# An attention block in which the score matmuls take all 128 rows of the array

## The chip, the cores and the metric

The kernel runs on one core of one Trainium2 chip. The metric is the device time of an execution in microseconds (us). Several executions are timed, and the median counts; one execution more is recorded by the hardware profiler, and its trace is what the profile and its views are read from.

Engines are named as in the profile: PE is TensorE (PEld are its weight loads), DVE is VectorE, ACT is ScalarE, POOL is GpSimd, SP is SyncE, which here only issues transfers. L188 is line 188 of the kernel.

## The reference, cut to what matters

The output mixes an attention block and a gated feed-forward block by a gate per token. There are 2048 tokens of width 448, and 16 heads of width 28.

```python
def _A_ref(x, wqkv, wo):                      # S = 2048, D = 448, H = 16, Dh = 28
    q, k, v = qkv[0], qkv[1], qkv[2]          # of x @ wqkv, by head
    scores = einsum("bhqd,bhkd->bhqk", q, k) * (Dh ** -0.5)
    p = softmax(scores)
    return einsum("bhqk,bhkd->bhqd", p, v) ... @ wo

def _B_ref(x, W_gate, W_up, W_down):          # F = 1792
    gate, up = x @ W_gate, x @ W_up
    return (gate * (gate > 0) * up) @ W_down

g = sigmoid((x * gate_w).sum(-1, keepdims=True))
return g * a + (1 - g) * b                    # a, b: the two blocks
```

## The kernel before

**Exactness by parts.** Most products are made in a faster 32-bit form of matmul with each operand split into a high part and a remainder. A projection is a chain of 11 matmuls (`TERMS`), issued at L341 for q and k and at L359 for v. The gate and up products of the feed-forward block are chains of the same kind at L510, the down product is at L770, the output projection at L725.

**Heads.** A head has only 28 rows, so four products of parts lie one below the other: `K[h % 3]` holds in rows 0 to 111 the parts high, low, high, low of k, and `Q[h]` the parts high, high, low, low of q. `GD` is 4 x 28 = 112. One matmul over 112 rows thus gives the sum of the four products. K has three buffers, Q three (tag "Q"). The rows 96 to 127 of each K buffer are filled with -1 at the start; the loads of a head overwrite rows up to 111, so rows 112 to 127 stay -1.

**Row maxima and scores.** For each head there are two passes over the 2048 x 2048 scores.

- `smax` (L188, L189): queries as weights, keys as moving data, 112 rows, into a bank of PSUM; VectorE reduces each 128 x 512 piece to maxima. There are 64 pieces a head. When a head is done, the maxima are transposed and split into two parts, which two small transfers on POOL's queue (L204) put into rows 112 and 113 of `Q[h]`.
- `scores` (L214, L216): keys as weights, queries as moving data, 114 rows. The two rows of maxima times the -1 in K subtract the maximum inside the product. ScalarE takes the exponential out of PSUM. There are 64 pieces a head, too.

The product with v follows per round (`pv`, L544) in column tiles of 32.

**Order.** The order of work on TensorE is written out by hand in strings of letters (`ROUNDS`): s is a matmul of scores, m one of row maxima, x one of gate or up. In most rounds they alternate. The row maxima run ahead of the scores by 24 tiles of keys and more. Weights for x come through `fetch_f` (SP's queue, L230) and are split by ScalarE and POOL.

**Loads of a head.** `load_k` (L174) and `load_q` (L179) issue four transfers each on SP's queue, 28 rows of 8 KB each. Heads 0, 1 and 2 are loaded during the projections and the first round; head h + 2 is loaded when the scores of head h begin, once the buffers of head h - 1 are free. SP issues its transfers in order.

**Start.** VectorE fills a small piece of V with zeros (L383); 11 matmuls on it keep TensorE going until data has come (L386). POOL then makes the identity, fills K with -1 (L393) and two columns of V per group (L395, L396), and is next used when the first q and k parts go out to DRAM (L348).

Of the kernel before, what the change touches and what calls it, by code (L numbers as in the profile page):

```python
# [8 lines left out]
F32 = mybir.dt.float32  # L9
# [9 lines left out]
P = 128  # L19
S = 2048  # L20
# [4 lines left out]
GD = G * DH  # L25
# [3 lines left out]
TB = 512  # L29
# [49 lines left out]
def gated_mix_kernel(ctx, tc, x, wq, wo, wgu, wd, out):  # L79
    nc = tc.nc  # L80
# [4 lines left out]
    dram = ctx.enter_context(tc.tile_pool(name="dram", bufs=1, space=DRAM))  # L85
# [4 lines left out]
    def f32(ap):  # L90
        return ap.bitcast(F32)
# [8 lines left out]
    def turn(kind, among):  # L100
        count[kind] = count.get(kind, -1) + 1
        return among[count[kind] % len(among)]
# [4 lines left out]
    def ps_x():  # L107
        return banks[turn("x", (4, 5))]
# [35 lines left out]
    x_d = {(tb, r): dram.tile([P, 4, TB], F32, name=f"x_d_{tb}_{r}") for tb in range(1, NB) for r in range(2)}  # L144

    v_d = {g: dram.tile([P, NK, 4, 32], F32, name=f"v_d_{g}") for g in (2, 3)}

    l_d = [dram.tile([NB, TB], F32, name=f"l_d_{h}") for h in range(H)]
    o_d = dram.tile([D, S], F32, name="o_d")
# [9 lines left out]
    V = vp.tile([P, 4, NK, 4, 32], F32, name="V")  # L159
    K = [vp.tile([P, S], F32R, name=f"K{r}") for r in range(3)]  # L160

    def p_slot(k, name, dt=F32):
        if k in (5, 6):
            return V[:, k - 3].rearrange("p k h d -> p (k h d)").rearrange("p (j t) -> p j t", t=TB)
        return (vp if k < 5 else att).tile([P, 4, TB], dt, name=name, tag=f"P{k}", bufs=1)
# [4 lines left out]
    Q = {}  # L170
# [5 lines left out]
    def load_q(h):  # L176
        Q[h] = q_slot(f"Q_{h}").rearrange("p j t -> p (j t)")
        for r in range(4):
            nc.sync.dma_start(f32(Q[h])[DH * r:DH * (r + 1)], qk_d[r // 2, 2 * DH * h + DH:2 * DH * (h + 1), :])  # L179

    MX, M = {}, {}

    def smax(k, ps):

        h, u, c = k // (4 * NK), k // 4 % NK, k % 4
        if u == 0 and c == 0:
            MX[h] = keep.tile([P, 64], F32, name=f"mx_{h}", tag="mx", bufs=2)
        nc.tensor.matmul(ps, Q[h][:GD, u * P:(u + 1) * P], K[h % 3][:GD, c * TB:(c + 1) * TB], start=True, stop=True)  # L188
        nc.vector.tensor_reduce(MX[h][:, 4 * u + c:4 * u + c + 1], ps, axis=AX.X, op=OP.max)  # L189
        if u == NK - 1 and c == 3:  # L190
            M[h] = keep.tile([P, 16], F32, name=f"m_{h}", tag="m", bufs=2)
            nc.vector.tensor_reduce(M[h], MX.pop(h).rearrange("p (a b) -> p a b", b=4), axis=AX.X, op=OP.max)
# [17 lines left out]
    def scores(i, j, ps):  # L210
        h, kt = divmod(i, NK)
        if j == 0:
            PT[i] = p_slot(i % NP, f"P_{i}")
        nc.tensor.matmul(ps, K[h % 3][:GD + 2, kt * P:(kt + 1) * P], Q[h][:GD + 2, j * TB:(j + 1) * TB],  # L214
                         start=True, stop=True)
        nc.scalar.activation(PT[i][:, j], ps, AF.Exp, scale=SCALE)  # L216

# [15 lines left out]
    with tc.tile_pool(name="qkv", bufs=1) as pa:  # L233
# [147 lines left out]

        warm = V[:, 3, 0:2].rearrange("p k h d -> p (k h d)").bitcast(BF16)
        nc.vector.memset(warm, 0.0)  # L383
        ps = ps_x()
        for n in range(WARM):
            nc.tensor.matmul(ps, warm[:, :P], warm, start=True, stop=True)  # L386
# [48 lines left out]
        for n, (f, *a) in enumerate(mixed):  # L435
            if n == 0:
                split_w(*w5)
            if n == 6:
                load_k(1)
                load_q(1)  # L440
            if n == 8:
                split_w(*w3)
            if n == 13:

                nc.gpsimd.memset(f32(K[2])[96:128], -1.0)
            if n == len(mixed) - 6:
                fetch_f(0)
            if n in spills:
                spill_x(*spills[n])

            among, ends = [], m
            while n >= first and m < (n + 1 - first) * ahead / (len(mixed) - first):
                among.append((smax, m, ps_w()))
                m += 1
            news = [(scores, *divmod(k, NB), ps_s()) for k, back in enumerate(EARLY) if back == len(mixed) - n]
            for k, c in enumerate(news):
                among.insert(2 * k + 1, c)
            f(*a, among=among)

            if 0 in M and ends >= 4 * NK:  # L460
                for part in smax_end(0, ps_x()):
                    part()
# [139 lines left out]
    for r, (order, nu) in enumerate(ROUNDS):  # L602
# [13 lines left out]
        for o in order:  # L616
            if o in "sS":
                i, j = i0 + ns // NB, ns % NB
                if j == 0 and i % 4 == 0:
                    small_things(i // 4)  # L620
                if len(EARLY) <= i * NB + j:
                    scores(i, j, ps_late(o) if o == "S" else ps_p() if late else ps_s())
                ns += 1
                if rest and ns > 2:
                    rest.pop(0)()
            elif o in "mM":
                smax(m, ps_late(o) if o == "M" else ps_w() if r == 0 and nm < 4 else ps_m())
                m += 1
                nm += 1
# [3 lines left out]
            elif o == "x":  # L633
                i, half, k = passes.pop(0)
# [3 lines left out]
                if k == NT - 1:  # L638
                    i, half, ps = units.pop()
# [231 lines left out]
```

## Time and profile before

| | us |
|---|---|
| median of 3 runs | 1284.22 |
| lowest and highest run | 1283.09, 1286.48 |
| the profiled execution | 1283.81 |
| its span in the profile | 1282.0 |

| engine | busy us | instructions |
|---|---|---|
| PE | 1275.8 | 6687 |
| PEld | 922.6 | 6687 |
| DVE | 895.3 | 1364 |
| ACT | 778.2 | 1424 |
| POOL | 371.2 | 563 |

Busy time is the time in which at least one instruction of the engine was under way. Matmuls overlap, one starting before the last has ended, so a busy TensorE does not tell the pace; for that the distance between starts is read. In a row of the groups, "112*128 112x512" stands for 112 rows and 128 columns of the array and 512 columns of moving data, then follow the count, the busy time of the group and the mean duration of one.

### The profile page before, as it was taken

The page shows a single profiled execution, that of the slowest core. Times are in us where ns is not written, and L with a number is a line of the kernel's source. Part 1 is how long each engine was busy: PE and PEld are TensorE (multiplying, and loading weights), DVE is VectorE, ACT ScalarE, POOL GpSimd, SP SyncE. Part 2 cuts the span into 40 slices and gives each one's busy share as a digit, 9 for nine tenths or more (in the row PEclk, how much of TensorE's full clock was granted, in tenths as well). Part 3 has the DMA queues.
Part 4 walks back from the last instruction along what each step waited for, and adds up shares of the span by engine and source line. Part 5 has one row for each costly group of instructions (what it writes and reads, how often), then busy time and mean ns, then how long its engine had stood idle before and what let it go on. Part 6 is the DMA issues. An engine that isn't in the chain of part 4 may idle for free.

```text
span 1282.0 us, 18203 instructions
## 1 busy us (share of the span) xinstructions
PE 1275.8 (100%) x6687; PEld 922.6 (72%) x6687; DVE 895.3 (70%) x1364; ACT 778.2 (61%) x1424; POOL 371.2 (29%) x563
## 2 busy tenths in 40 slices
PE   9999999999999999999999999999999999999998
PEld 6888866677666676666766667766677666899997
DVE  6598768798777897777977779877788314753342
ACT  5212767686766786677867668766787774322121
POOL 3222222412333122423133331324222443641020
PEclk9999999999999999999999999999999999999999
DMA  9936443133144314141444323142331225644432
GB/s 314 297 148 243 138 128 94 63 83 102 59 120 159 75 43 115 66 107 43 123 109 131 97 60 90 52 115 66 91 107 47 86 84 176 203 129 158 133 114 79
DMA packets 53569, 148.89 MB, mean 116 GB/s; under 512 B 10024, under 2 KB 17128, under 8 KB 48872
## 3 DMA queue, kind: packets, MB, share of 16 engines
q1 hardware_dynamic: 36120, 98.34, 26.9%
q0 software_dynamic: 16928, 48.93, 10.6%
q8 instruction: 52, 0.85, 0.3%
q10 hardware_dynamic: 432, 0.46, 0.1%
q14 instruction: 37, 0.30, 0.1%
HBM read 102.06 MB, written 46.02 MB: 116 GB/s over the span
## 4 chain that ended last, share of the span: by engine, by line
PE 99%; DMA 0%; ACT 0%; DVE 0%; SPq 0%; issue 0%; ACTq 0%
PE b L510 22%; PE b L214 19%; PE b L188 19%; PE b L544 17%; PE b L770 10%; PE b L341 6%; PE b L359 3%; PE b L725 3%; DMA wr<-wq 0%; PE b L196 0%; DVE wg L136 0%; ACT wg L130 0%; SPq L293 0%; DVE y L776 0%; ACT W L130 0%
## 5 line engine op out<-in xcount | busy, mean ns | idle before, releaser
L189 DVE TENSOR_REDUCE mx<-b 128x1 f32<-128x512 f32 x1024 | 685.7, 688 | 28.7 <-PE b L188 20.4
L216 ACT ACTIVATE P<-b 128x512 f32<-128x512 f32 x840 | 493.9, 599 | 153.8 <-PE b L214 84.6
L510 PE MATMUL b<-X,wg 128*128 128x512 f32 (+1 forms) x1232 | 438.1, 400 | 0.3 <-DVE wg L136 0.3
L214 PE MATMUL b<-Q,K 114*128 114x512 f32 x1024 | 406.9, 397 | 0.0
L188 PE MATMUL b<-K,Q 112*128 112x512 f32 x1024 | 403.7, 397 | 0.0
L510 PEld LDWEIGHTS b<-X,wg 128*128 128x128 f32 (+1 forms) x1232 | 222.5, 189 | 58.7 <-issue 9.5
L214 PEld LDWEIGHTS b<-Q,K 114*128 114x128 f32 x1024 | 194.4, 190 | 55.0 <-issue 12.6
L188 PEld LDWEIGHTS b<-K,Q 112*128 112x128 f32 x1024 | 193.1, 189 | 48.6 <-DVE mx L189 2.7
L544 PE MATMUL b<-P,V 128*32 128x512 f32 x1680 | 188.2, 593 | 0.0
L139 POOL TENSOR_TENSOR wg<-wgr,wg 128x384 fp32r<-128x384 f32 x200 | 143.4, 732 | 9.8 <-issue 1.6
L544 PEld LDWEIGHTS b<-P,V 128*32 128x32 f32 x1680 | 52.6, 110 | 121.2 <-issue 118.7
L770 PE MATMUL b<-WD,hh 128*128 128x448 f32 x672 | 138.5, 365 | 0.0
L532 POOL DMA_DIRECT2D h_d<-h x56 | 31.4, 562 | 363.0 <-DVE h L526 312.0
L770 PEld LDWEIGHTS b<-WD,hh 128*128 128x128 f32 x672 | 126.2, 188 | 10.3
L216 ACT ACTIVATE V<-b 128x512 f32<-128x512 f32 x184 | 107.9, 600 | 41.5 <-PE b L214 26.8
L130 ACT ACTIVATE hh<-hr 128x512 fp32r<-128x512 f32 x56 | 35.4, 631 | 124.4 <-PE b L770 120.2
L136 DVE TENSOR_TENSOR hh<-hr,hh 128x512 fp32r<-128x512 f32 x56 | 50.1, 894 | 66.1 <-ACT hh L130 66.1
L341 PE MATMUL b<-X,W 128*128 128x512 f32 x308 | 84.3, 398 | 0.6 <-ACT X L130 0.6
L550 DVE TENSOR_TENSOR os<-b,os 128x512 f32<-128x512 f32 x16 | 11.1, 692 | 86.1 <-PE b L544 86.1
L341 PEld LDWEIGHTS b<-X,W 128*128 128x128 f32 x308 | 57.9, 189 | 15.4 <-DVE X L136 1.7
L559 POOL DMA_DIRECT2D l_d<-rs x16 | 9.0, 561 | 203.5 <-DVE rs L558 203.5
L548 DVE COPY os<-b 128x512 f32<-128x512 f32 x16 | 11.1, 691 | 78.5 <-PE b L544 78.5
(70 smaller groups left out, 710.9 us busy)
## 6 DMA issues: line engine op xcount, KB each, us to landing
wgr<-wgu SPq DMA_DIRECT2D x55, 512.0 KB
K<-qk_d SPq DMA_DIRECT2D x64, 224.0 KB
Q<-qk_d SPq DMA_DIRECT2D x64, 224.0 KB
h_d<-h POOLq DMA_DIRECT2D x56, 256.0 KB, 2.6
hr<-h_d SPq DMA_DIRECT2D x56, 256.0 KB
qk_d<-st POOLq DMA_DIRECT2D x21, 512.0 KB, 3.6
x_d<-X POOLq DMA_DIRECT2D x6, 1024.0 KB, 5.1
X<-x_d SPq DMA_DIRECT2D x24, 256.0 KB
```

The costliest lines, as they stand in the source:

```text
L136: nc.vector.tensor_tensor(dst, src, f32(high), op=OP.subtract)
L139: nc.gpsimd.tensor_tensor(dst, src, f32(high), op=OP.subtract)
L188: nc.tensor.matmul(ps, Q[h][:GD, u * P:(u + 1) * P], K[h % 3][:GD, c * TB:(c + 1) * TB], start=True, stop=True)
L189: nc.vector.tensor_reduce(MX[h][:, 4 * u + c:4 * u + c + 1], ps, axis=AX.X, op=OP.max)
L214: nc.tensor.matmul(ps, K[h % 3][:GD + 2, kt * P:(kt + 1) * P], Q[h][:GD + 2, j * TB:(j + 1) * TB], start=True, stop=True)
L216: nc.scalar.activation(PT[i][:, j], ps, AF.Exp, scale=SCALE)
L341: nc.tensor.matmul(ps, W[:, a, c * P:(c + 1) * P], xf(tb, b), start=(n == 0), stop=(n == NT - 1))
L359: nc.tensor.matmul(ps[:, :VC], xf(tb, b)[:, t * P:(t + 1) * P], W[:, a, 2 * D:2 * D + VC], start=(n == 0), stop=(n == NT - 1))
L510: nc.tensor.matmul(ps, WS[i][rows, s, a], xf(i // NF, b)[rows], start=(n == 0), stop=(n == NT - 1))
L544: nc.tensor.matmul(po[32 * j:32 * j + 32], V[:, h // 4 % 2, i % NK, h % 4], p[:, j], start=(i == i0), stop=(i == i0 + ni - 1))
L725: nc.tensor.matmul(ps[:, :D], ON[tb][b // 4][:, b % 4, t * P:(t + 1) * P], WO[:, a], start=(n == 0), stop=(n == NT - 1))
L770: nc.tensor.matmul(ACC[i // NF][t][:, :D], HH[i][:, a, t * P:(t + 1) * P], WD[:, f, b], start=(f == 0 and n == 0), stop=(f == NF - 1 and n ...
```

## The change

The matmuls of `smax` and of `scores` read all 128 rows of K and Q in place of the first 112 and 114. Rows 112 to 127 of K hold -1 as before. Rows 112 to 127 of Q, which held no defined values but the maxima, are filled with zeros with each load of a head, by a fifth transfer on SP's queue, which reads a row of zeros in DRAM (`z_d`) 16 times. That row is written once at the start by a transfer on POOL's queue, from the zeros that VectorE has put into V for the first matmuls. The maxima are later written over rows 112 and 113 as before.

```diff
+    z_d = dram.tile([1, S], F32, name="z_d")
...
         for r in range(4):
             nc.sync.dma_start(f32(Q[h])[DH * r:DH * (r + 1)], qk_d[r // 2, 2 * DH * h + DH:2 * DH * (h + 1), :])
+        nc.sync.dma_start(f32(Q[h])[GD:], z_d[0:1].to_broadcast([P - GD, S]))
...
-        nc.tensor.matmul(ps, Q[h][:GD, u * P:(u + 1) * P], K[h % 3][:GD, c * TB:(c + 1) * TB], start=True, stop=True)
+        nc.tensor.matmul(ps, Q[h][:, u * P:(u + 1) * P], K[h % 3][:, c * TB:(c + 1) * TB], start=True, stop=True)
...
-        nc.tensor.matmul(ps, K[h % 3][:GD + 2, kt * P:(kt + 1) * P], Q[h][:GD + 2, j * TB:(j + 1) * TB],
+        nc.tensor.matmul(ps, K[h % 3][:, kt * P:(kt + 1) * P], Q[h][:, j * TB:(j + 1) * TB],
                          start=True, stop=True)
...
         nc.vector.memset(warm, 0.0)
+        nc.gpsimd.dma_start(z_d.rearrange("a (p c) -> (a p) c", p=8), V[:8, 3, 0:2].rearrange("p k h d -> p (k h d)"))
```

The order of the instructions on TensorE, VectorE and ScalarE is the same before and after. SP has 16 transfers more, POOL one.

## The prediction

> **What bounds the kernel now.** I read the page first: the busy shares, the granted clock, the chain that ended last. Then I read the groups by line with shapes kept apart, and last the timeline, since a change in the shape of a matmul is paid for in the distance from one start to the next.
>
> ```profile
> span 1282.0 us, 18203 instructions
> ...
> PE 1275.8 (100%) x6687; PEld 922.6 (72%) x6687; DVE 895.3 (70%) x1364; ACT 778.2 (61%) x1424; POOL 371.2 (29%) x563
> ...
> PEclk9999999999999999999999999999999999999999
> ...
> PE 99%; DMA 0%; ACT 0%; DVE 0%; SPq 0%; issue 0%; ACTq 0%
> PE b L510 22%; PE b L214 19%; PE b L188 19%; PE b L544 17%; PE b L770 10%; PE b L341 6%; PE b L359 3%; PE b L725 3%; DMA wr<-wq 0%; PE b L196 0%; DVE wg L136 0%; ACT wg L130 0%; SPq L293 0%; DVE y L776 0%; ACT W L130 0%
> ```
>
> TensorE is busy for all but 6.2 us of the span, at the full granted clock, and the chain that sets the end runs through it for 99%. The two lines that the change rewrites, L188 and L214, hold 38% of that chain. So two things can move the time: a different pace of these matmuls, or a new wait in front of TensorE. Work on other engines and queues costs nothing as long as TensorE never waits for it.
>
> **Term 1: the matmuls get 128 rows.** The change replaces 1024 matmuls of 112 rows and 1024 of 114 rows by as many of 128 rows. Columns stay at 512, weight columns at 128, and the order of instructions on TensorE is the same, so no instruction is added there.
>
> ```profile
> L510 PE MATMUL b<-X,wg 128*128 128x512 f32 x1136 | 421.7, 396 | 0.3 <-DVE wg L136 0.3
> L214 PE MATMUL b<-Q,K 114*128 114x512 f32 x1024 | 406.9, 397 | 0.0
> L188 PE MATMUL b<-K,Q 112*128 112x512 f32 x1024 | 403.7, 397 | 0.0
> L510 PEld LDWEIGHTS b<-X,wg 128*128 128x128 f32 x1136 | 215.3, 190 | 50.0 <-DVE mx L189 1.5 <-DVE wg L136 0.9 <-issue 0.8
> L188 PEld LDWEIGHTS b<-K,Q 112*128 112x128 f32 x1024 | 193.1, 189 | 48.6 <-DVE mx L189 2.7
> ```
>
> A matmul of 128 rows lasts 396 ns, one of 114 or 112 rows 397; the weight loads last 190 and 189. By duration the row count is free. But matmuls overlap, so duration is not pace. For pace I take two stretches of 20 us with no column-tiled work in them: at 18 us every matmul has 128 rows, at 300 us the three shapes alternate. The first two rows are stretches (length, busy time and instructions by engine, granted clock, DMA share, GB/s), the others are the TensorE groups inside them.
>
> ```profile
> 18.00:38.00 20.00, 20.00 (x88) 16.20 (x87) 13.20 (x20) 10.96 (x20) 6.44 (x9) 1.00 1.00 362
> 300.00:320.00 20.00, 20.00 (x87) 16.18 (x86) 19.67 (x30) 17.06 (x29) 0.00 (x0) 1.00 0.40 93
> ...
> L341 PE MATMUL b<-X,W 128*128 128x512 f32 x88 | 20.6, 395 | 0.0
> ...
> L510 PE MATMUL b<-X,wg 128*128 128x512 f32 x29 | 11.5, 397 | 0.0
> L214 PE MATMUL b<-Q,K 114*128 114x512 f32 x29 | 11.5, 396 | 0.0
> L188 PE MATMUL b<-K,Q 112*128 112x512 f32 x29 | 11.5, 396 | 0.0
> ```
>
> 88 against 87: with the 0.40 us that the last one hangs over, 20.4/88 = 232 ns against 20.4/87 = 234.5 ns, and one matmul more or less at an edge is 2.7 ns. So the paces agree as closely as this can say. Longer runs of starts are sharper (rows of the timeline, and two of the chain, "8.07" and "1075.10"):
>
> ```profile
> 10.80 27.47 PE L341 MATMUL b<-X,W 128*128 128x512 f32 x117
> ...
> 300.17 0.40 PE L510 MATMUL b<-X,wg 128*128 128x512 f32 x1
> 300.40 0.39 PE L188 MATMUL b<-K,Q 112*128 112x512 f32 x1
> 300.63 0.40 PE L214 MATMUL b<-Q,K 114*128 114x512 f32 x1
> ...
> 302.97 0.40 PE L510 MATMUL b<-X,wg 128*128 128x512 f32 x1
> ...
> 1087.58 5.20 PE L510 MATMUL b<-X,wg 128*128 128x512 f32 x22
> ...
> 8.07 30.20 PE b L341 x126
> ...
> 1075.10 10.21 PE b L510 x44
> ```
>
> The mix: twelve starts from 300.17 to 302.97, 233.3 ns each; a step out of 128 rows, one out of 112 and one out of 114 all take 0.23 to 0.24. Full rows alone: (27.47 - 0.40)/116 = 233.4 ns early in the kernel, 10.21/44 = 232.0 and (5.20 - 0.40)/21 = 228.6 near the end. The early stretch, nearest in kind since the other engines and the DMAs are at work around it, gives the pace of the mix to 0.1 ns. I take 0 for this term. Its bounds: a gain if the mix went at the fastest full-row pace, 234.5 - 228.6 = 5.9 ns; a loss if the new matmuls went at the slowest full-row stretch shown, 30.20/126 = 239.7 ns (which holds start-up waits), so 5.2 ns.
>
> **Term 2: sixteen zero loads on SP's queue.** Each head's load of Q gets a fifth transfer, 16 rows of 8 KB, 128 KB, behind its four of 224 KB. The maxima of a head now need it too. Head 0 has the least room:
>
> ```profile
> Q<-qk_d SPq DMA_DIRECT2D x64, 224.0 KB
> ...
> 42.87 4.41 SPq L174 DMA_DIRECT2D K<-qk_d  x4
> 48.66 3.52 SPq L179 DMA_DIRECT2D Q<-qk_d  x4
> ...
> SPq L179 <- DMA Q<-qk_d: 3.6, 4, 1.4
> ...
> 52.88 0.19 PEld L188 LDWEIGHTS b<-K,Q 112*128 112x128 f32 x1
> ```
>
> The four Q loads of head 1 (48.66) were each held until a Q load of head 0 had landed (the waits row). Their issues end at 48.66 + 3.52 = 52.18; with 0.44 us for one issue (1.76/4 in a row further down) the last left at 51.74, so head 0's Q was in by then, and one follows another at (3.52 - 0.44)/3 = 1.03 us. The zeros come next in the queue, where K of head 1 was (42.87). At 128/224 of 1.03 us they land 0.59 us later, at 52.33; the first weights of L188 are read at 52.88. They fit by 0.55 us: cost 0. If they took as long as a whole load they would land at 52.77 and still fit; two loads long would cost 0.9 us.
>
> The Trainium skill, "SBUF — State Buffer", section on the DMA port swizzle, says that bandwidth follows the number of ports that the partitions reach, and that 16 partitions reach four, with 104 GB/s measured. By that the transfer would take 1.26 us, an estimate from that page, the zeros would land at 53.00, and the sum would be 0.1 us more. No row of this trace has a 16-partition load of this size.
>
> Later heads have room:
>
> ```profile
> 284.31 0.22 DVE L192 TENSOR_REDUCE m<-mx 128x16 f32<-128x64 f32 x1
> ...
> 255.69 1.76 SPq L179 DMA_DIRECT2D Q<-qk_d  x4
> 290.33 0.36 SPq L230 DMA_DIRECT2D wgr<-wgu  x1
> ```
>
> Head 4's Q is issued at 255.69 to 257.45. Its first maximum comes after head 3's maxima are closed at 284.31. In SP's queue nothing goes out after that load until 290.33. A transfer of 0.44 us issue and 0.6 us data disappears in 27 us. Where SP's next transfer follows closer (head 1's loads behind head 0's, the gate weights behind head 2's), what is queued is delayed by about 0.5 to 1 us and is used many microseconds later. The waits of L510 for its weights add up to 0.3 us (L510's row above). Cost 0.
>
> **Term 3: the zeros themselves, on POOL's queue.** One transfer of 8 KB goes out ahead of all of POOL's own start-up work, and waits for the memset of V on VectorE. Behind it wait the identity, the two fills of K and the fills of V; the last fills of V also wait for its landing, since they overwrite what it reads.
>
> ```profile
> 0.74 0.20 POOL masks.py:197 MEMSET ident<- 128x128 f32 x1 [0.29 <-POOLq L864]
> ...
> 0.87 0.27 DVE L383 MEMSET V<- 128x256 uint32 x1 [0.87 <-PEq L864]
> ...
> 5.38 2.06 PE L341 MATMUL b<-X,W 128*128 128x512 f32 x6
> ...
> 6.84 0.21 POOL L396 MEMSET V<- 128x64 f32 x1
> 12.59 0.89 POOL L348 DMA_DIRECT2D qk_d<-st  x1 [5.54 <-DVE st L136]
> ...
> rb<-l_d POOLq DMA_DIRECT2D x64, 64.0 KB, 2.2
> ```
>
> The memset is over at 1.14. POOL, whose first fill began at 0.74, is then late by 0.40 for the wait and up to 0.89 for the issue (as long as the one at 12.59), 1.3 us; and before 12.59 it stands idle for 5.54 us. A small POOL transfer lands after a median of 2.2 us, so the zeros are in by 1.14 + 0.89 + 2.2 = 4.2 us, before the last fills, which end at 6.84. Without that idle time it would cost 1.3 us. Cost 0. The two transfers per head that put the row maxima into Q, POOL's too, now also wait for the zeros and for L188's reads; both are long over when the maxima exist. Cost 0.
>
> **Sum.** The profiled execution took 1283.81 us for its span of 1282.0. Change 0 + 0 + 0, so 1283.8 there. The median of the three runs, 1284.22, is 0.4 above it; the forecast is that median, **1284.2 us**. The likeliest case's own range is 1281 to 1287: the three runs spread from 1283.09 to 1286.48, a pace off by 0.5 ns over the 3052 matmuls of the mix is 1.5 us, and 1.3 us stands for POOL's start.
>
> **Rivals.** *Full rows are faster.* If the alternation of 128, 112 and 114 rows is what keeps the mix at 234.5 ns, the whole mix gains: the 2048 changed matmuls and the 1004 of L510 between them (1136 less six blocks of 22 at the end). At 232.0 ns that is 3052 x 2.5 = 7.6 us, 1276.6; at 228.6 it is 18 us, 1266. For it: no full-row run in the late stage is slower than the mix. Against it: the run of 117, and what a real change of rows looks like:
>
> ```profile
> 599.30 0.39 PE L188 MATMUL b<-K,Q 112*128 112x512 f32 x1
> 599.62 0.73 PE L510 MATMUL b<-X,wg 64*128 64x512 f32 x4
> ```
>
> Going to 64 rows costs 0.32 us from start to start, 0.09 more than any step among 112, 114 and 128. Those three behave as one mode. The Trainium skill, "TensorEngine Tiling (Array Packing)", Key Properties, says that changing the tiling mode, not just the tile, drains the engine; by that rule this rival would hold only if 112 and 114 rows were modes of their own, and the trace shows the drain at 64 rows alone. Chance 0.20.
>
> *Full rows are slower.* Each of the 2048 changed matmuls takes a few ns more, because 14 or 16 more rows are fed. It counts as slower from 1.9 ns (3.9 us); at 5.2 ns it is 10.6 us, 1294.8. Against it: the group durations and the run of 117. Chance 0.10.
>
> *The zeros of head 0 are late.* Place: TensorE at 52.88, in front of the first L188; the whole in-order engine stands. A load of 28 rows in 1.03 us, with at most two rows to each of the 16 DMA engines, is 0.51 us a row; if all 16 rows ran through one engine they would take 8.2 us, land at 59.9 and cost 7.1 us, 1291.3. It counts as slower from a landing at 56.8. Against it: the loads of 28 rows from the same queue, which go at a pace that one engine can't have. Chance 0.06.
>
> **How the numbers follow.** No effect 0.64, full rows faster 0.20, full rows slower 0.10, zeros late 0.06. A measurement of this kernel can tell about 0.3% from no change, 3.9 us. That makes 0.20 faster, 0.64 same, 0.16 slower. For the range I take the likeliest case and the nearer part of each rival: 1275 to 1290 leaves out roughly 0.08 of the first rival and 0.09 of the other two.
>
> **What would show it.** Right: the stretch at 300 us again with 87 or 88 matmuls, both groups near 397 ns, VectorE's and ScalarE's rows unchanged, no wait of L188's weight load for a DMA at 53 us. Term 1 is wrong if three alternating starts take less than 0.690 us or more than 0.712 us; term 2 if TensorE shows a gap before its first row maximum or before a later head; term 3 if TensorE's first projections start later than 5.38 us.

## The result: 0.8% faster, and the profile after

| | before | after |
|---|---|---|
| median of six runs, us | 1284.35 | 1274.68 |
| lowest and highest run, us | 1282.88, 1286.48 | 1272.70, 1276.21 |
| span of the profiled execution, us | 1282.0 | 1272.5 |

The ratio is 0.9922, with an interval of 0.9910 to 0.9934. The forecast was no change; the time that came is near that of the rival that full rows are faster. The page of the changed kernel, in the parts that were shown of the one before:

```profile
span 1272.5 us, 18233 instructions
...
PE 1265.0 (99%) x6687; PEld 915.9 (72%) x6687; DVE 891.1 (70%) x1364; ACT 776.3 (61%) x1424; POOL 371.3 (29%) x564
...
PEclk9999999999999999999999999999999999999999
...
PE b L514 21%; PE b L217 19%; PE b L191 19%; PE b L548 18%; PE b L774 10%; PE b L344 5%; PE b L362 3%; PE b L729 3%; DMA wr<-wq 0%; DVE WD L133 0%; PE b L199 0%; DVE hh L136 0%; DVE wg L136 0%; DVE WO L133 0%; DVE W L136 0%
...
L192 DVE TENSOR_REDUCE mx<-b 128x1 f32<-128x512 f32 x1024 | 681.5, 687 | 23.7 <-PE b L191 19.5
...
L514 PE MATMUL b<-X,wg 128*128 128x512 f32 (+1 forms) x1232 | 434.6, 397 | 1.9 <-DVE wg L136 1.9
L217 PE MATMUL b<-Q,K 128*128 128x512 f32 x1024 | 403.3, 394 | 0.0
L191 PE MATMUL b<-K,Q 128*128 128x512 f32 x1024 | 401.2, 395 | 0.0
```

Lines have moved by 3 to 4: the row maxima are L191 now, the scores L217, gate and up L514. TensorE is still the whole chain at the full granted clock, with the same 6687 matmuls. A matmul of L217 or L191 lasts 394 or 395 ns in place of 397, but since they overlap that doesn't tell the pace. The time is in the distances between starts. First the stretch at 18 us, where all matmuls had 128 rows already, then the one at 300 us, then 800 us of the rounds; in a fence of its own the same 800 us of the kernel before:

```profile
18.00:38.00 20.00, 20.00 (x88) 16.25 (x87) 13.21 (x20) 11.14 (x21) 6.53 (x9) 1.00 1.01 370
300.00:320.00 20.00, 20.00 (x91) 15.66 (x89) 19.25 (x28) 16.93 (x30) 0.00 (x0) 1.00 0.44 98
200.00:1000.00 800.00, 800.00 (x4424) 533.12 (x4423) 629.55 (x974) 584.66 (x1061) 237.63 (x392) 1.00 0.35 91
```

```profile
200.00:1000.00 800.00, 800.00 (x4362) 536.27 (x4364) 634.85 (x976) 585.01 (x1057) 228.91 (x378) 1.00 0.31 87
```

88 matmuls at 18 us as before; 91 in place of 87 at 300 us (the stretch doesn't hold quite the same work, since all is earlier now); 4424 in place of 4362 over 800 us. Single starts, the first and the last of a run, in the rounds that have all three kinds and in the late rounds that have scores and gate products alone:

```profile
299.70 0.39 PE L217 MATMUL b<-Q,K 128*128 128x512 f32 x1
...
303.87 0.40 PE L217 MATMUL b<-Q,K 128*128 128x512 f32 x1
...
1046.12 0.39 PE L217 MATMUL b<-Q,K 128*128 128x512 f32 x1
...
1048.62 0.62 PE L514 MATMUL b<-X,wg 128*128 128x512 f32 x2
```

Eighteen steps from 299.70 to 303.87 are 231.7 ns each, against 233.3 before. Eleven from 1046.12 to 1048.62 are 227.3. The same eleven before:

```profile
1046.26 0.40 PE L214 MATMUL b<-Q,K 114*128 114x512 f32 x1
...
1048.83 0.63 PE L510 MATMUL b<-X,wg 128*128 128x512 f32 x2
```

233.6 ns. Matching every start of the one trace with the same matmul of the other shows where the 9.5 us of the span come from: 0.5 us in the first 17 us (start-up), nothing from 17 to 53 us, 1.0 us from there to 146 us, 8.3 us in the rounds up to 1000 us, 1.3 us in the late rounds to 1066 us, and 1.5 us are given back after that.

In what follows, *pace* is the mean distance between neighbouring starts from 146 to 1000 us, over the steps that lie between 200 and 260 ns, some 2640 to 2720 of them in each trace (this leaves out steps into and out of the column-tiled products and the 64-row ones). Before it is 234.06 ns, after 230.54.

### The profile page after: what moved, and what is told of

Its sections match the earlier page's. It is cut to its first block, busy times and chain, and to the rows that moved or that the text cites. A ratio compares the mean times of both kernels' runs of the same rounds, so it can differ in the third digit from the quotient of the medians.

```text
span 1272.5 us, 18233 instructions
## 1 busy us (share of the span) xinstructions
PE 1265.0 (99%) x6687; PEld 915.9 (72%) x6687; DVE 891.1 (70%) x1364; ACT 776.3 (61%) x1424; POOL 371.3 (29%) x564
## 4 chain that ended last, share of the span: by engine, by line
PE 98%; DVE 1%; issue 0%; DMA 0%; ACT 0%; DVEq 0%
PE b L514 21%; PE b L217 19%; PE b L191 19%; PE b L548 18%; PE b L774 10%; PE b L344 5%; PE b L362 3%; PE b L729 3%; DMA wr<-wq 0%; DVE WD L133 0%; PE b L199 0%; DVE hh L136 0%; DVE wg L136 0%; DVE WO L133 0%; DVE W L136 0%
## 5 line engine op out<-in xcount | busy, mean ns | idle before, releaser
L192 DVE TENSOR_REDUCE mx<-b 128x1 f32<-128x512 f32 x1024 | 681.5, 687 | 23.7 <-PE b L191 19.5
L514 PE MATMUL b<-X,wg 128*128 128x512 f32 (+1 forms) x1232 | 434.6, 397 | 1.9 <-DVE wg L136 1.9
L217 PE MATMUL b<-Q,K 128*128 128x512 f32 x1024 | 403.3, 394 | 0.0
L191 PE MATMUL b<-K,Q 128*128 128x512 f32 x1024 | 401.2, 395 | 0.0
L514 PEld LDWEIGHTS b<-X,wg 128*128 128x128 f32 (+1 forms) x1232 | 220.2, 188 | 57.4 <-issue 9.5
L191 PEld LDWEIGHTS b<-K,Q 128*128 128x128 f32 x1024 | 191.8, 187 | 54.6 <-DVE mx L192 3.5
L217 PEld LDWEIGHTS b<-Q,K 128*128 128x128 f32 x1024 | 192.3, 188 | 48.7 <-issue 12.6
L136 DVE TENSOR_TENSOR hh<-hr,hh 128x512 fp32r<-128x512 f32 x56 | 46.8, 835 | 66.2 <-ACT hh L130 66.2
```

The costliest lines, as they stand in the source:

```text
L136: nc.vector.tensor_tensor(dst, src, f32(high), op=OP.subtract)
L191: nc.tensor.matmul(ps, Q[h][:, u * P:(u + 1) * P], K[h % 3][:, c * TB:(c + 1) * TB], start=True, stop=True)
L217: nc.tensor.matmul(ps, K[h % 3][:, kt * P:(kt + 1) * P], Q[h][:, j * TB:(j + 1) * TB], start=True, stop=True)
L514: nc.tensor.matmul(ps, WS[i][rows, s, a], xf(i // NF, b)[rows], start=(n == 0), stop=(n == NT - 1))
```

## The experiments

Two explanations were open. *Alternation*: a matmul whose row count differs from its neighbour's costs time, and the change makes all counts equal. *Full rows*: a matmul of 128 rows is faster as such. Beside these stood what the zero transfers do. All runs are edits of the changed kernel, except one of the kernel before. "Rows" are those of maxima, scores, gate and up. Each ratio is to runs of the kernel before in the same series, whose median lay between 1283.9 and 1284.8 us.

| run | rows | median us | ratio to before, interval | pace ns |
|---|---|---|---|---|
| before | 112, 114, 128 | 1284.35 | 1 | 234.06 |
| after | 128, 128, 128 | 1274.68 | 0.9922 [0.9910, 0.9934] | 230.54 |
| loads_only | 112, 114, 128 | 1284.61 | 1.0004 [0.9994, 1.0014] | 233.97 |
| maxima_only | 128, 114, 128 | 1282.44 | 0.9990 [0.9974, 1.0005] | 233.37 |
| scores_only | 112, 128, 128 | 1280.37 | 0.9976 [0.9963, 0.9988] | 233.57 |
| uniform_114 | 114, 114, 128 | 1282.60 | 0.9990 [0.9980, 0.9999] | 233.20 |
| all_112 | 112, 112, 112 | 1279.12 | 0.9957 [0.9942, 0.9972] | 230.51 |
| x_112 | 128, 128, 112 | 1284.38 | 1.0003 [0.9992, 1.0014] | 233.20 |
| rows_96 | 96, 96, 128 | 1281.54 | 0.9981 [0.9972, 0.9991] | 233.12 |
| rows_127 | 127, 127, 128 | 1282.63 | 0.9989 [0.9980, 0.9999] | 233.19 |
| max_448 | 128, 128, 128 | 1263.74 | 0.9839 [0.9824, 0.9854] | 227.23 |
| before_max_448 | 112, 114, 128 | 1281.92 | 0.9980 [0.9970, 0.9989] | 233.48 |
| eighth_114 | one in 24: 114 | 1267.09 | 0.9855 [0.9838, 0.9871] | 228.19 |
| quarter_114 | one in 12: 114 | 1269.78 | 0.9877 [0.9858, 0.9897] | 229.18 |
| one_112 | 128, one at the end 112 | 1273.40 | 0.9909 [0.9896, 0.9923] | 230.50 |
| last_block_112 | 128, eleven at the end 112 | 1275.48 | 0.9931 [0.9906, 0.9956] | 230.09 |
| better | 128, 128, 128 | 1273.33 | 0.9916 [0.9903, 0.9928] | 230.52 |

### The zero transfers alone

```diff
# loads_only
-matmul(ps, Q[h][:, u * P:(u + 1) * P], K[h % 3][:, c * TB:(c + 1) * TB], ...)
+matmul(ps, Q[h][:GD, u * P:(u + 1) * P], K[h % 3][:GD, c * TB:(c + 1) * TB], ...)
...
-matmul(ps, K[h % 3][:, kt * P:(kt + 1) * P], Q[h][:, j * TB:(j + 1) * TB], ...)
+matmul(ps, K[h % 3][:GD + 2, kt * P:(kt + 1) * P], Q[h][:GD + 2, j * TB:(j + 1) * TB], ...)
```

> The zero transfers of the change, with the matmuls left at 112 and 114 rows. If the row count makes the gain (either by the alternation of counts or by partial rows), this is as slow as before: 1284 us within 1.5, and 12 starts of the mix again take about 2.80 us (233 ns each). If the transfers or the place of something in memory make it, this is as fast as after: 1275 us, 231 ns or less.

With the transfers and the old row counts the time and the pace are those of before. Its stretch of the rounds holds three matmuls more than before in 4362:

```profile
200.00:1000.00 800.00, 800.00 (x4365) 536.08 (x4367) 634.49 (x976) 584.22 (x1057) 229.09 (x378) 1.00 0.34 90
```

So the gain comes from the row counts, not from a transfer that moves something else.

### One of the two lines at a time, and both at one other count

```diff
# maxima_only: maxima with all rows, scores as before
+matmul(ps, K[h % 3][:GD + 2, ...], Q[h][:GD + 2, ...], ...)
# scores_only: scores with all rows, maxima as before
+matmul(ps, Q[h][:GD, ...], K[h % 3][:GD, ...], ...)
# uniform_114: both lines
+... [:GD + 2, ...] ...
```

> Row maxima over 128 rows, scores over 114. Alternation theory (each step from one row count to another costs a few ns): two of three steps in the mix still change the count, so a third of the 10 us gain comes, about 1281 us, and the late rounds without maxima (114 against 128 rows) stay at 233 ns. Partial-row theory, each partial matmul pays for itself: half of the gain, 1279.5 us. Partial-row theory with a pace that one slow shape sets for all: no gain in the mix, 1283 to 1284 us.

> Scores over 128 rows, row maxima over 112. Alternation theory: a third of the gain in the mix (two of three steps still change the count) and all of it in the late rounds, about 1280 us. Partial-row theory, each pays for itself: half of the gain and all of the late rounds' 1.3 us, 1279 us. One slow shape sets the pace of all: 233 ns in the mix and 227 ns in the late rounds, 1282 to 1283 us.

> Row maxima and scores both over 114 rows (rows 112 and 113 of Q are zero while the maxima are made). Alternation theory: the step from maxima to scores no longer changes the count, a third of the gain, about 1281 us. Partial-row theory: both shapes are still partial, no gain, 1284 us, mix at 233 ns.

If full rows were faster as such, half the change would bring half of the 3.5 ns. It brings 0.5 to 0.7 ns, a fifth at most, and making maxima and scores equal at 114 brings 0.9. The simple form of alternation, a fixed price for each step that changes the count, was off too: it promised a third of the gain for each of the three, 1280 to 1281 us, and only scores_only came near (1280.37). As long as one kind in three differs, the pace stays at 233 to 234 ns. The late rounds say the same more sharply, since they hold scores and gate products alone: there scores_only, whose two kinds are equal, has 227.0 ns as the changed kernel has, while maxima_only and uniform_114 have 233.3 as before (means of the starts from 1000 to 1066 us).

### Equal counts without full rows, and the other way round

```diff
# all_112: maxima and scores [:GD], and gate and up
-        rows = slice(0, P)
+        rows = slice(0, GD)
# x_112: gate and up alone
-        rows = slice(0, P)
+        rows = slice(0, GD)
```

> Row maxima, scores and the gate and up products (except their closing half-row terms) all over 112 rows: in the rounds no step changes the row count, but every matmul is partial. Left out: 16 rows of each feed-forward product, and the subtraction of the maxima. Alternation theory: the rounds run at the pace of after (mean 230.5 ns from 146 to 1000 us, 227 in the late rounds), about 1275 to 1276 us, since only the first stage still mixes 112 with 128. Partial-row theory: 233 to 234 ns in the rounds and the late rounds, 1283 to 1285 us.

> Maxima and scores over 128 rows as in after, the gate and up products over 112 (16 rows of each left out). If a partial shape in the mix is enough, whichever line it is on: 233 ns in the rounds and in the late rounds, about 1283 us; in the first stage, before the gate products begin, the pace of after. If the gain belongs to the score matmuls alone (their operands K and Q): 230.5 ns in the rounds, 1275 us.

This pair decides. With no maxima, scores, gate or up product of 128 rows, but equal counts, the rounds run as in the changed kernel; with maxima and scores full, but gate and up at 112, they run at 233.2. The stretch of all_112, then that of x_112:

```profile
200.00:1000.00 800.00, 800.00 (x4425) 533.29 (x4425) 630.46 (x976) 584.41 (x1062) 237.28 (x392) 1.00 0.34 91
```

```profile
200.00:1000.00 800.00, 800.00 (x4383) 534.54 (x4385) 633.91 (x976) 584.93 (x1058) 230.97 (x381) 1.00 0.34 90
```

4425 matmuls, against the changed kernel's 4424; 4383 in x_112. Full rows as such fall; alternation stands. The total of all_112 is 4.4 us above the changed kernel's all the same. That difference is not in the rounds. Before 146 us its trace gains 0.9 us less than the changed kernel's; there maxima of 112 rows still alternate with projections of 128. After 1066 us it loses 6.3 us against that of before, the changed kernel's 1.5: 3.2 us in the projections (below), and 3.1 in the last gate chains, where TensorE waited 1.8 us and the granted clock was 0.92 from 1080 to 1090 us and 0.95 in the 20 us behind.

```diff
# rows_96: maxima and scores
+... [:96, ...] ...
# rows_127: maxima and scores
+... [:127, ...] ...
```

> Maxima and scores over 96 rows, three quarters of the array with none begun; left out are the last part products and the subtraction of the maxima. If only a row count that leaves a block of 32 rows begun costs: the pace of after, 230.5 ns and 227 in the late rounds, 1275 us. If any count under 128 costs: 233 to 234 ns and 1284 us; if less rows cost in proportion, more than that, some 1290 us.

> Maxima and scores over 127 rows, one short of after. If any count under 128 costs the same: 233 to 234 ns in the rounds, 233 in the late rounds, 1284 us. If the cost goes with the number of rows left out: as after within 0.5 ns, 1275 us.

One row short of 128 costs what 32 rows short cost: 233.19 and 233.12 ns. So it is not the number of rows, and not whether it is a multiple of 32; it is that the count differs. Weights and moving data change their count together in all these runs; which of the two costs is not told apart.

### How the cost of a differing count is paid

```diff
# quarter_114 (eighth_114: "j == 0 and kt % 2 == 0"), both with the shorter reduction of the next part
+        rows = GD + 2 if j == 0 else P
-matmul(ps, K[h % 3][:, kt * P:(kt + 1) * P], Q[h][:, j * TB:(j + 1) * TB], ...)
+matmul(ps, K[h % 3][:rows, kt * P:(kt + 1) * P], Q[h][:rows, j * TB:(j + 1) * TB], ...)
```

> The changed kernel with two edits: VectorE's maximum reads 448 of 512 columns (left out: 64 columns of each row-maximum piece), as in the run with the shorter reduction, so that VectorE isn't the bound; and every fourth score matmul has 114 rows again, so that among 12 matmuls of a round there is one of 114 rows, with one change into it and one out of it. Reference points: 1263.7 us and a mean start-to-start of 227.2 ns with no such matmul; 1281.9 us and 233.5 ns where every matmul differs from the one before. (A) each change costs what it does where all differ, 6.3 ns: two in twelve are 1.1 ns on the mean, 228.3 ns, 1267 us. (B) a change costs the 15 to 25 ns that the single one at the end of the feed-forward block showed: 2.5 to 4 ns on the mean, 230 to 231 ns, 1271 to 1275 us. (C) one differing matmul puts the whole neighbourhood into the slow pace: 233 ns, 1281 us.

> As the run with every fourth score matmul at 114 rows, but every eighth of them alone in alternate tiles of keys: one matmul of 114 rows among 24. VectorE reads 448 of 512 columns (64 left out). (A) 227.7 ns, 1265 us. (B) 228.4 to 229.2 ns, 1267 to 1269 us. (C), where the neighbourhood is at least 24 matmuls long: still 233 ns, 1281 us; where it is shorter, a bimodal sequence of steps.

One differing matmul in 12 adds 1.95 ns to the mean step (229.18 against 227.23 without it), one in 24 adds 0.96. That is 23 ns for each differing matmul, both times: so far apart, the costs add up. 23 ns for a change in and a change out, some 12 for each, lies between the cases (A) and (B) written down (6.3, and 15 to 25, for each); (C), a whole neighbourhood at 233 ns, falls. Two score matmuls that are twelve steps apart, first in quarter_114 from one of 114 rows to the next, then in max_448:

```profile
268.08 0.40 PE L218 MATMUL b<-Q,K 114*128 114x512 f32 x1
...
270.83 0.40 PE L218 MATMUL b<-Q,K 114*128 114x512 f32 x1
```

```profile
266.18 0.39 PE L217 MATMUL b<-Q,K 128*128 128x512 f32 x1
...
268.90 0.39 PE L217 MATMUL b<-Q,K 128*128 128x512 f32 x1
```

2.75 us against 2.72. The starts of quarter_114, taken to the ns, show how this is spread: the steps are 226 or 227 ns, the one into a 114-row matmul too, but for the four that begin with it: 232 or 233 from its start to the next, then 237 or 238, 232 or 233, and 231, together some 27 over 226.7 (23 against the mean of 227.23, which holds slower steps of its own). This fits that equal neighbours inside a mixed sequence were slow as well: a differing matmul slows the step that it begins and the three behind it. Where every third matmul differs, the mean step is 233.1 to 233.6, some 6.7 ns over the 226.7; one price of 23 ns in three steps would be 7.7, so neighbouring costs overlap.

### What holds the changed kernel above 226.7 ns

The changed kernel's steps in the rounds are not even. In a stretch where the three kinds alternate VectorE reduces one piece to every three matmuls. A reduction takes 687 ns (L192's row); three steps of 226.7 are 680. In both kernels the reduction was cut to 448 of the 512 columns:

```diff
# max_448 (of the kernel after), before_max_448 (of the kernel before)
-nc.vector.tensor_reduce(MX[h][:, 4 * u + c:4 * u + c + 1], ps, axis=AX.X, op=OP.max)
+nc.vector.tensor_reduce(MX[h][:, 4 * u + c:4 * u + c + 1], ps[:, :448], axis=AX.X, op=OP.max)
```

> As after, but VectorE reduces only 448 of each 512 scores to a maximum (the last 64 of each piece left out), about 0.62 us instead of 0.688 us. If what is left above 226.7 ns in the rounds of after (230.5 ns) is VectorE, whose one reduction of 688 ns must fit in three matmuls of 3 x 226.7 = 680 ns: the rounds fall to 227 ns, 2640 matmuls x 3.6 ns = 9 us less, about 1265 us. If it is the rhythm of TensorE disturbed by something else: 230.5 ns again, 1275 us.

> As before (112 and 114 rows), with the same shorter reduction. Control: if the row counts hold TensorE at 233.3 ns (700 ns for three, more than VectorE's 688), a shorter reduction changes little, 233 to 234 ns and 1283 to 1284 us. If VectorE was the bound before as well: 227 to 230 ns and under 1278 us.

```profile
200.00:1000.00 800.00, 800.00 (x4471) 544.61 (x4470) 589.48 (x979) 594.42 (x1080) 241.38 (x397) 1.00 0.34 92
```

```profile
200.00:1000.00 800.00, 800.00 (x4384) 539.58 (x4387) 585.50 (x975) 585.05 (x1057) 230.94 (x382) 1.00 0.32 88
```

The first row is max_448, the second before_max_448. VectorE's busy time falls by some 40 to 50 us in both, but the kernel before gains 2.4 us from it, and the changed one 10.9. VectorE's timeline of the changed kernel, of max_448 and of the kernel before, each a run of reductions without a break:

```profile
299.21 6.24 DVE L192 TENSOR_REDUCE mx<-b 128x1 f32<-128x512 f32 x9
```

```profile
299.09 6.06 DVE L192 TENSOR_REDUCE mx<-b 128x1 f32<-128x448 f32 x9
```

```profile
299.42 5.63 DVE L189 TENSOR_REDUCE mx<-b 128x1 f32<-128x512 f32 x8
```

From start to start that is (6.24 - 0.69)/8 = 694 ns after, (6.06 - 0.62)/8 = 680 with the short reduction, which is three matmuls of 226.7, and (5.63 - 0.69)/7 = 706 before, which is three of 235. Over the rounds from 146 to 1000 us the median distance is 692 after, 680 with the short reduction and 700 before, and VectorE's median idle time between two reductions 2, 55 and 8 ns. Before, TensorE set this distance and VectorE had a little room. After, VectorE sets it, a little above its own 687. So the equal row counts are worth 18.2 us by themselves (1281.92 to 1263.74, with VectorE out of the way), and the changed kernel gets 9.7 of them.

### After the rounds: what is given back

Once the gate products are done, TensorE works on down and output projections of 448 columns. There x_112 and all_112 lost time, though all their matmuls have 128 rows there. Two runs ask how little of another count is enough:

```diff
# one_112
+        if i == NB * NF - 1 and s and n == NT - 1:
+            rows = slice(0, GD)
# last_block_112
+        if i == NB * NF - 1 and s:
+            rows = slice(0, GD)
```

> As after, but one matmul of 6687, the last of the last gate and up block, has 112 rows (16 rows of one term of that block left out). Only down products and output projections over 128 rows follow it. If a change of row count is paid at the step itself: nothing to see, the tail at 202.7 ns a matmul and 1275 us. If a change puts TensorE into a slower rhythm that stays until something resets it (as the tail of the kernel with gate products over 112 rows suggests, 206.7 ns there to the end): 206.7 ns from that matmul on, some 840 matmuls, 3.3 us more, 1278 us.

> The changed kernel with the last 22 gate and up matmuls at 112 rows (left out: the last 16 of their 128 rows of products). All other matmuls of the kernel before and after them have 128 rows. One change in and one out, with a block between. If a block of 112 rows leaves something behind, the 128-row matmuls of 448 columns after it stay at 206.7 ns from start to start, as in the runs with all gate and up matmuls at 112 rows, and the time is some 3 us above the changed kernel's 1274.7, so 1277 to 1278. If not, they return to 202.7 ns after a few matmuls, and the time is 1274.7.

The edit of last_block_112 reaches the last chain of eleven, not the 22 that were written down. Groups of twelve down projections behind the last gate block, in the order after, x_112, one_112, last_block_112:

```profile
1110.76 2.59 PE L774 MATMUL b<-WD,hh 128*128 128x448 f32 x12
```

```profile
1107.99 5.18 PE L514 MATMUL b<-X,wg 112*128 112x512 f32 x22
1113.00 2.64 PE L774 MATMUL b<-WD,hh 128*128 128x448 f32 x12
```

```profile
1110.00 2.59 PE L776 MATMUL b<-WD,hh 128*128 128x448 f32 x12
```

```profile
1109.00 2.64 PE L776 MATMUL b<-WD,hh 128*128 128x448 f32 x12
```

2.59 us or 2.64: a step of 202.7 or of 206.7 ns. One 112-row matmul leaves 202.7 behind it, after three slower steps; eleven in a row leave 206.7, and that holds for the following 800 steps up to the end, long after the last differing count. That is 3.2 us in last_block_112. Its time, 1275.48 us, is below the 1277 to 1278 that were written down for this case all the same: its trace has no wait like the one below. Of the 17 traces, the three whose last gate chain has 112 rows throughout have 206.7 ns to the end, all others 202.7. What the engine keeps so long is not settled; a block of another count as the last thing ahead of these projections is enough for it.

The changed kernel has no such block; what its trace gives back is a wait:

```profile
1078.48 4.75 DVE L133 CAST WD<-wdr 128x448 fp32r<-128x448 f32 x1
1079.86 4.39 POOL L139 TENSOR_TENSOR WO<-wor,WO 128x1344 fp32r<-128x1344 f32 x2
...
1083.98 0.39 PE L514 MATMUL b<-X,wg 128*128 128x512 f32 x1
1086.25 5.06 PE L514 MATMUL b<-X,wg 128*128 128x512 f32 x21 [1.89 <-DVE wg L136]
```

VectorE's cast of a piece of `WD`, which takes 0.38 to 0.39 us in most of its 14 instances, takes 4.75 us while POOL splits `WO`, and the weights that VectorE splits next come 1.9 us late for TensorE. The Trainium skill, "SBUF — State Buffer", section "Who interferes with whom", says that VectorE and GpSimd share one pair of ports as an exclusive lock; these two rows agree with it in kind, though the cast begins 1.4 us ahead of POOL's row.

The gain does not bring this wait, though. The kernel before has the same stop beside the split of `WO`, on a later instruction of VectorE, and TensorE waits 0.3 us there; and loads_only, with the row counts of before and none of the gain, has the cast of 4.75 us and the wait. The stop of the kernel before, then TensorE's wait in loads_only:

```profile
1089.39 4.85 DVE L136 TENSOR_TENSOR hh<-hr,hh 128x512 fp32r<-128x512 f32 x1
```

```profile
PE b L514 <- DVE wg L136: 1.9, 1, 1.9
```

Each of the other traces but that of the run "better" has one such stop, of 4.1 to 4.9 us: where it falls on the cast, TensorE waits 1.4 to 1.9 us (after, loads_only, uniform_114, all_112, max_448, before_max_448, eighth_114, one_112), elsewhere 0.6 at most. What decides where it falls was not tried, and one trace a kernel can't tell whether it changes from execution to execution.

A last run shortened what POOL holds at a time, and sent the zeros of head 0 ahead of its other loads:

```diff
# better
-        dve_high(WO[:, 0:3], wor[:, 0:3])
-        pool_low(WO[:, 3:6], wor[:, 0:3], WO[:, 0:3])
+        for c in range(3):
+            dve_high(WO[:, c], wor[:, c])
+            pool_low(WO[:, 3 + c], wor[:, c], WO[:, c])
...
+        zeros_q(0)               # the transfer of zeros, ahead of load_k(0); later heads: ahead of load_q(h)
         load_k(0)
         load_q(0)
```

> As after, with the zeros of head 0 issued ahead of its K loads, of later heads ahead of their Q loads, and the split of the output weights in pieces of 448 columns, so that POOL does not hold VectorE back for 4.7 us at once. If the wait of 1.9 us at the head of the tail comes from that split and the waits of 1.1 to 1.3 us for Q of head 0 that two of the runs showed come from the zeros queued behind it: both gone, 1272 us. If not: 1275 us.

```profile
1079.38 2.72 DVE L133 CAST WD<-wdr 128x448 fp32r<-128x448 f32 x1
```

The cast is down to 2.72 us, and TensorE's wait to 1.1. The time, 1273.33 us, is not to be told from the changed kernel's: the two intervals overlap. It missed the 1272 that were expected.

## Why the prediction was wrong

**Term 1 failed**, and with it the sum. The prediction took 0 ns for the row counts, bounded by -5.9 and +5.2 ns on each of the 3052 matmuls. The measured change of pace is -3.5 ns, inside the bounds; the 0 taken from them is what failed, and with VectorE out of the way it would have been off by more (233.5 to 227.2). It went wrong at two places.

First, the run of 117 full-row matmuls was taken as the pace of full rows, since it matched the mix to 0.1 ns. That match was a coincidence. The same projections in the changed kernel, which has full rows everywhere in its rounds too, are as slow as they were:

```profile
8.55 29.26 PE L344 MATMUL b<-X,W 128*128 128x512 f32 x124 [0.28 <-DVE X L136]
```

(29.26 - 0.40)/123 = 234.6 ns, while the same kernel's late rounds go at 227.0. Start by start it repeats every eleven steps, which is one chain of a projection, between 226 and 241 ns. So another sequence of matmuls has a pace of its own; what slows this one was not tried. The fast reference, 228.6 ns near the end, was seen and set aside because the other stretch was "nearest in kind".

Second, "those three behave as one mode" was read from the 0.09 us that a step to 64 rows costs. That is the wrong test: a small cost that every step of the mix pays looks the same as none, and the mix had no step without a change beside it to compare with. At 6.7 ns a step the cost is far below 0.09 us, and still a large part of what the kernel can gain. The sign that was to show term 1 wrong, three starts in less than 0.690 us, was set too far off as well: the pace of the changed kernel gives 3 x 230.5 = 692 ns. The count of matmuls at 300 us, 91 in place of 87 or 88, did show it. The Trainium skill, "TensorEngine Tiling (Array Packing)", Key Properties, speaks of a drain when the tiling mode changes. By the runs a change of count between 128 and 127 rows costs too, 6.5 ns a step; whether that is a small drain no run here shows.

The rival *full rows are faster* gave 1276.6 us at 232.0 ns and 1266 at 228.6. The first is near: 1274.7, at 230.5. The condition it was tied to, that the alternation keeps the mix slow, is what all_112 and x_112 show; its name is wrong, since all_112 has none of these matmuls at 128 rows and the same pace. The second would have come about had VectorE not become the bound: max_448 has 227.2 ns and 1263.7 us. The prediction quoted VectorE at 19.67 us busy of 20 at 300 us and didn't ask what a faster TensorE would run into.

**Term 2** took 0 for the zeros, and loads_only measures 0 (1.0004). In the changed kernel the first weights of L191 are read at 52.55 us, 0.33 us earlier than before, and no wait of TensorE for a transfer is listed there. The margin of 0.55 us is not there, though: the wait for the zeros, an entry of its own in TensorE's queue, ended at 52.31 us, near the 52.33 worked out, and the weights were read with nothing to spare. These are TensorE's waits on Q of head 0 in maxima_only, x_112 and quarter_114 (us in total, times, longest):

```profile
PE b L191 <- DMA Q<-qk_d: 1.1, 1, 1.1
```

```profile
PE b L191 <- DMA Q<-qk_d: 1.3, 1, 1.3
```

```profile
PE b L191 <- DMA Q<-qk_d: 1.0, 1, 1.0
```

In last_block_112 and eighth_114 the same matmul is 0.6 and 0.2 us late. So it costs between nothing and 1.3 us from run to run, with the same transfers. The 0.9 us written down for "two loads long" lies in that range. The 0.1 us estimated from the Trainium skill, "SBUF — State Buffer", section on the DMA port swizzle, does so too. With the zeros sent first, the run "better" has no such wait. The rows name the whole of Q, but the entries of TensorE's queue tell its parts apart: in x_112 the wait for the zeros ends at 53.95 us, in maxima_only at 53.52, and the next entry, for the last load of q, takes 0.05 us. So the zeros came last. The loads of q ahead of them were late too: by the landings in the traces, the last of them was in at 53.16 us in x_112, 0.75 us ahead of the zeros, against 51.86 in the kernel before.

**Term 3** holds: cost 0. POOL's fills of K start at 2.75 us in place of 1.38, as late as worked out (1.3 us), behind this row:

```profile
1.45 0.65 POOL L387 DMA_DIRECT2D z_d<-V  x1 [0.99 <-DVE V L386]
```

POOL's idle time ahead of its first transfer of q and k falls from 5.54 to 3.51 us, and takes it up. TensorE's first projections start at 5.51, later than the 5.38 that was to show this term wrong; but loads_only, with POOL equally late, has 5.39, so POOL isn't the reason.

**The sum** has no term for the stretch after 1066 us, where 1.5 us were lost. Since uniform_114 and before_max_448, whose counts still differ, lose 1.5 and 1.4 us there, and loads_only 3.2, it is not an effect of equal counts; what brings it is open.

## What to carry to other kernels

Where matmuls of different row counts alternate, try to make the counts equal (zeros against finite values in the other operand), even at the price of rows that compute nothing: a differing matmul cost some 23 ns of TensorE's time here. Judge a pace only against the same matmuls in the same place, and ask of a run of other work that happens to match why it does. Before costing a faster engine, look at the next busiest in that very stretch: VectorE, at 98% there, took half of this gain.

## What was not expected of the hardware

- Row counts of 96, 112, 114 and 127 next to 128 cost the same, 233.1 to 233.6 ns a step in place of 226.7; all at 112 cost nothing (226.9 ns in the late rounds, the changed kernel 227.0). One differing matmul is felt over the four steps that begin with it, 23 ns in sum.
- A last chain of eleven matmuls of 112 rows ahead of 800 matmuls of 128 rows and 448 columns left those at 206.7 ns a step instead of 202.7, to the end of the kernel; a single one didn't. Why isn't known.
